# An attention and SwiGLU layer on one core: the paired P V of chunks 2 to 4 moved ahead by 10, 12 and 26 column blocks

## The chip, the cores and the metric

The kernel runs on one core of a Trainium2 chip. The metric is the device time of one execution in microseconds (us). The engines of the core are TensorE (PE in the profile, its weight loads PEld), VectorE (DVE), ScalarE (ACT), GpSimd (POOL) and SyncE (SP). Each works through its own list of instructions in order, and they wait for each other by semaphores. SP and ACT also issue DMA transfers, each through a queue of its own.

## The reference

The input x has 2048 rows of 576 values, in bf16. It is normalised once, and two branches read the result. The output is x plus both branches.

```python
xn = _layernorm(x)
# branch A: attention, H = 32 heads of Dh = 18, a window of W = 256 keys
qkv = (xn @ wqkv).reshape(B, S, 3, H, Dh)
scores = einsum("bhqd,bhkd->bhqk", q, k) * Dh ** -0.5
mask = (i - j >= 0) & (i - j < W)
A = einsum("bhqk,bhkd->bhqd", softmax(where(mask, scores, -1e9)), v) -> (B, S, D) @ wo
# branch B: gated MLP, F = 4608
h = silu(xn @ w1) * (xn @ w3)
B = h @ w2
return x + A + B
```

## The kernel before, in words

The 2048 rows are worked in four chunks of 512 (`CH`; the code counts them `c` = 0 to 3, the text 1 to 4). The 32 heads lie in eight groups of four (`G`). A chunk has these stages:

- **Units.** The loop `for u in range(NF)` (line 1391) makes 36 units of the gated MLP. A unit is 128 of the 4608 columns of gate and up. `unit_pairs` (line 851) issues it as nine **column blocks** (`for n in range(9)`, line 1399), each a pair of matmuls, one in each half of the array; one matmul reads `xnT`, or its copy with the halves swapped, `xnS`. Behind the nine blocks `unit_tanh` (ACT, line 869) and `unit_h` (two operations on DVE, lines 875 and 878) turn the two PSUM banks of the unit into a row block of `hT`. Three pairs of banks, handed out in turn by `job()`, serve the units.
- **Score steps among the units.** In chunks 2 to 4, attention groups 4 to 7 are worked here, five steps for a group, 20 in all. A step is `scores` (PE, line 682), `exps` (ACT, line 691) and `masks` (POOL, line 718). `spaced_step` (line 1367) sets them apart: a clock counts column blocks and steps, and the steps left share the blocks left up to `ALL_DONE[c]`, though never closer than 7.5. The exponentials lie in buffers: two slots of `stage`, the four buffers of W2 (`w2`), the slots `pt` and the buffers `od`.
- **The joint.** At block `n` of unit `u`, with `(u, n) = JOINTS[c]` (line 1401), both P V of the chunk are issued behind each other: `pv(c, 2, ...)` and `pv(c, 3, ...)` (line 739), 96 short matmuls each. They use the two pairs of banks that the current unit doesn't use. No score step falls in the eight blocks ahead (`calm`, line 1305), and all 20 steps must be done. The four transposes out of PSUM follow on DVE (`pv_out`, line 800), then the scaling on POOL (`o_scale`, line 806) and the transposes back (`o_turn`, line 813), dealt by `later` to the units `u` to `u + 5`. `o_pack` (line 817), four DMA issues on SP which wait for those transposes, moves the first pair into `oT` at `u + 3`; that of the second pair is put at `NF + 6` in chunks 2 and 3, and at `u + 6` in chunk 4.
- **W2's first pieces.** They go into the buffers `w2`, which hold exponentials until the first P V has read them. Line 1485 issues one in each of up to four units behind the joint, after that unit's last matmul:

```python
if joint[0] < u < joint[0] + 5:
    load_w2(c * 2 * NFC + 4, (op,))
```

- **Projections of the next chunk** (chunks 1 to 3, line 1504 on). `xn_swap` (line 460) copies `xnT` to `xnS` by two DMAs, once the last unit has read the old `xnS`; if fewer than four pieces of W2 have been issued, the rest is issued right behind it (line 1510). What `later` has dealt to units past the last comes out here, at item `m` for `u <= NF + m`. Then come the projections to queries, keys and values (`proj_part`, line 496), and the DMAs that deal them out: keys `new_k` on SP (line 638), queries `new_q` on ACT (four copies, line 625).
- **Lanes** (`w2_lanes`, chunks 1 to 3). The product with W2 runs in four row strips of the array at once (line 1036); among its rounds stand the score steps of the *next* chunk's groups 0 to 3 (line 756), which read `qv` and `kn`, and their P V (line 791). The first step is due 2.2 us into the stage (`W2_FIRST`). The last chunk has no next one and runs `p2_list` instead (line 932).

SP also loads the gate and up weights, a pair of parts at a time (`load_part`, line 343), by what the units owe: two parts behind every fourth unit, issued at blocks 3 and 8 of the unit that follows. In chunk 4 the last pair goes out in unit 24, and x of the chunk is loaded at unit 29 (`load_four`, line 315). The order of each engine's list is fixed when the program is written; nothing is chosen while it runs.

## Time and profile before

| | |
|---|---|
| median of three runs | 558.03 us (557.88 to 558.33) |
| the profiled execution's own time | 557.89 us |
| its span, from first to last instruction | 556.1 us |
| PE busy | 548.5 us (99%) |
| DVE, ACT, POOL busy | 364.5, 294.9, 120.4 us |
| time that PE's waits take by the list of waits | 1.8, 1.4, 1.2 and 0.6 us |
| start of the projections behind chunks 2 and 3 | 237.92 and 376.47 us |

A row of a timeline or of the chain gives the start in us from the start of the span, the length, the engine, the line of the kernel, the operation with `out<-in`, and how many were merged; in brackets stands the idle time just before it and what ended it. "issue" means that the engine waited for nothing that the profile shows. A row of a DMA view with 40 digits gives the busy share of the DMA engines in 40 equal slices of the stretch, in tenths. Queue q8 carries PE's instructions. A busy PE is a modelled figure, since matmuls overlap: the step from one row's start to the next is the better measure of pace.

### The profile page before, as it was taken

The numbers are of one execution on the slowest core, as the hardware profiler recorded it, in microseconds if no ns is written. First come the engines' busy times: TensorE is split into PE (matmuls) and PEld (weight loads), VectorE is DVE, ScalarE is ACT, GpSimd is POOL, SyncE is SP. The second block draws the span as 40 slices with busy tenths as digits, with TensorE's granted clock in tenths as the row PEclk, the third lists the DMA queues.
The fourth block names the chain that finished last, engine by engine and source line by source line (L and its number), as shares of the span: only waits on it lengthen the run. The fifth ranks groups of instructions, "written<-read, shape, count | busy, mean of one in ns | idle before, by whom it ended". The sixth has DMA issues, their size and how long they took to land.

```text
span 556.1 us, 17660 instructions
## 1 busy us (share of the span) xinstructions
PE 548.5 (99%) x7690; PEld 314.0 (56%) x7690; DVE 364.5 (66%) x745; ACT 294.9 (53%) x481; POOL 120.4 (22%) x281
## 2 busy tenths in 40 slices
PE   8999999999999999998999999999999999999998
PEld 4786554565564444565656444456555544444776
DVE  7566988746648787763665888676466676669011
ACT  6457766368826555246873565533786466533000
POOL 5524545100013422110001243202000232211000
PEclk9999999999999999999999999999999999999999
DMA  9997999559699999465979999937697989844552
GB/s 246 201 201 145 207 188 193 117 115 158 137 187 200 192 188 156 94 145 114 150 142 193 194 198 179 168 61 171 118 171 130 190 179 172 158 88 142 136 150 64
DMA packets 166070, 88.12 MB, mean 158 GB/s; under 512 B 101546, under 2 KB 163754, under 8 KB 165994
## 3 DMA queue, kind: packets, MB, share of 16 engines
q1 hardware_dynamic: 164622, 85.42, 81.2%
q10 hardware_dynamic: 1372, 1.59, 1.2%
q8 instruction: 60, 0.98, 0.8%
q14 instruction: 16, 0.13, 0.1%
HBM read 71.30 MB, written 2.36 MB: 132 GB/s over the span
## 4 chain that ended last, share of the span: by engine, by line
PE 98%; DMA 1%; issue 0%; ACT 0%; DVE 0%
PE ps L860 51%; PE ps L1036 16%; PE ps L496 9%; PE ps L932 6%; PE ps L682 4%; PE ps L1086 2%; PE ps L739 2%; PE ps L1045 2%; PE ps L756 2%; PE ps L791 2%; DMA qv<-stage 1%; PE ps L1160 1%; PE ps L939 1%; PE ps L1096 0%; PE ps L440 0%
## 5 line engine op out<-in xcount | busy, mean ns | idle before, releaser
L860 PE MATMUL ps<-xnT,w 64*128 64x512 bf16 x1400 | 179.3, 376 | 0.0
L860 PE MATMUL ps<-xnS,w 64*128 64x512 bf16 x1120 | 149.1, 376 | 0.6 <-issue 0.6
L875 DVE SCALAR_TENSOR_TENSOR gs<-thb,ps 128x512 bf16<-128x512 bf16 x144 | 97.8, 679 | 62.6 <-ACT thb L869 62.0
L869 ACT ACTIVATE thb<-ps 128x512 bf16<-128x512 f32 x144 | 85.7, 595 | 74.5 <-PE ps L860 72.9
L860 PEld LDWEIGHTS ps<-xnT,w 64*128 64x128 bf16 x1400 | 71.6, 94 | 67.4 <-DVE ofin L800 0.2
L1036 PE MATMUL ps<-hT,w 32*128 32x512 bf16 x1728 | 107.3, 374 | 0.0
L878 DVE SCALAR_TENSOR_TENSOR hT<-gs,ps 128x512 bf16<-128x512 bf16 x144 | 98.9, 687 | 5.0
L860 PEld LDWEIGHTS ps<-xnS,w 64*128 64x128 bf16 x1120 | 57.2, 94 | 55.7 <-issue 1.5
L1036 PEld LDWEIGHTS ps<-hT,w 32*128 32x128 bf16 x1728 | 59.3, 92 | 27.2 <-issue 1.4
L763 ACT ACTIVATE pt<-ps 128x512 bf16<-128x512 f32 x120 | 65.0, 595 | 9.8 <-PE ps L756 9.6
L691 ACT ACTIVATE pt<-ps 128x1024 bf16<-128x1024 f32 (+1 forms) x46 | 46.2, 1004 | 34.9 <-PE ps L682 34.8
L756 PE MATMUL ps<-qv,kn 18*128 18x384 bf16 (+2 forms) x288 | 54.6, 267 | 1.8 <-DMA qv<-stage 1.8
L806 POOL TENSOR_TENSOR oq<-uq,rden 128x288 bf16<-128x288 f32 x12 | 8.1, 672 | 189.4 <-DVE rden L805 189.4
L771 DVE TENSOR_TENSOR pt<-pt,kv 128x256 int32<-128x256 int32 x96 | 31.3, 371 | 26.6 <-ACT pt L763 26.1
L718 POOL TENSOR_TENSOR pt<-pt,mk 128x128 int32<-128x128 int32 (+1 forms) x82 | 33.1, 424 | 53.7 <-ACT pt L691 53.6
L496 PE MATMUL ps<-xnT,wp 64*128 64x512 bf16 (+1 forms) x360 | 38.5, 355 | 0.0
L932 PE MATMUL ps<-w,hT 128*128 128x288 bf16 (+1 forms) x292 | 36.9, 284 | 0.0
L756 PEld LDWEIGHTS ps<-qv,kn 18*128 18x128 bf16 x288 | 26.5, 93 | 16.7 <-issue 2.3
L932 PEld LDWEIGHTS ps<-w,hT 128*128 128x128 bf16 x292 | 28.2, 98 | 7.4 <-issue 0.5
L682 PE MATMUL ps<-qv,kv 64*128 64x320 bf16 (+4 forms) x336 | 32.1, 258 | 0.0
L813 DVE STREAM_TRANSPOSE od<-oq 128x256 bf16<-128x256 bf16 x64 | 25.5, 425 | 6.5 <-POOL oq L806 6.5
L990 DVE TENSOR_TENSOR thb<-ps,thb 128x512 f32<-128x512 f32 x24 | 16.6, 692 | 18.5 <-ACT thb L987 17.9
(132 smaller groups left out, 534.0 us busy)
## 6 DMA issues: line engine op xcount, KB each, us to landing
w<-in_B_w_dram SPq DMA_DIRECT2D x60, 576.0 KB, 7.5
w<-in_B_w_dram SPq DMA_DIRECT2D x72, 288.0 KB, 4.1
w<-in_B_w_dram SPq DMA_DIRECT2D x12, 192.0 KB, 6.8
xp<-in_A_x_dram SPq DMA_DIRECT2D x4, 576.0 KB, 5.0
xnS<-xnT SPq DMA_DIRECT2D x8, 256.0 KB, 4.8
xp<-in_A_x_dram SPq DMA_DIRECT2D x14, 144.0 KB, 4.4
oT<-od SPq DMA_DIRECT2D x56, 36.0 KB
w<-in_B_w_dram SPq DMA_DIRECT2D x6, 320.0 KB, 5.1
```

What stands on the lines that cost most here:

```text
L496: op = add("pe", lambda e, out_=out_, st=st, mv=mv, n=n, r0=r0, first=first: e.matmul(out_, st, mv, start=first, stop=(part == 1 and n == ...
L682: add("pe", lambda e, r0=r0, out_=out_, kb=kb, q0=q0, nb=nb: e.matmul(out_, kb4[r0:r0 + 64, g - GN, kb + NV - NB, :] if kb < 0 else kv[r0: ...
L691: add("act", lambda e: e.activation(pt_slot(sl)[:, 0:w, :], PS[:, SC[0]:SC[1] + 1, 0:w].rearrange("p r q -> p q r"), ACT.Exp, scale=scale) ...
L718: add("pool", lambda e, vb=vb, mm=mm: e.tensor_tensor(vb, vb, mm, ALU.mult), r=(key if n == 0 else []) + ["mk"], **{"w" if n == 0 else "j" ...
L756: add("pe", lambda e: e.matmul(PS[:, b, c0:c0 + nb * 128], kn[32 * a:32 * a + Dh, g, W + 128 * jb:W + 128 * jb + 128], qv[32 * a:32 * a + ...
L763: add("act", lambda e: e.activation(head_of(sl, p), PS[:, b, :], ACT.Exp, scale=scale), r=[("ps", b)], **{"j" if p else "w": pt_keys(sl)})
L860: op = add("pe", lambda e, n=n, r0=r0, r=r, k=k, src=src: e.matmul(PS[:, b0 + r, :], wt[r0:r0 + 64, k, fl * 128:(fl + 1) * 128], src, star ...
L869: add("act", lambda e: e.activation(th[i][:], PS[:, bg, :], ACT.Tanh, scale=0.5), r=[("ps", bg)], w=[("th", i)])
L875: add("dve", lambda e: e.scalar_tensor_tensor(out=gs[i][:], in0=th[i][:], scalar=1.0, in1=PS[:, bg, :], op0=ALU.add, op1=ALU.mult), r=[("t ...
L878: add("dve", lambda e: e.scalar_tensor_tensor(out=hT[:, u, :], in0=gs[i][:], scalar=0.5, in1=PS[:, bu, :], op0=ALU.mult, op1=ALU.mult), r= ...
L932: add("pe", lambda e: e.matmul(bank, hT[:, f, tt * 128:(tt + 1) * 128], w2[sl][:, k, n0:n1], start=first, stop=(c + 1 == NC and half == 1 ...
L1036: add("pe", lambda e, b=b, rows=rows, wt=wt, fl=fl, k=k, a=a, first=first: e.matmul(PS[:, b, :], wt[rows, fl, :], hT[rows, k, :], start=fi ...
```

## The change

The joints of chunks 2, 3 and 4 stand at other places, and the blocks by which the score steps are to be done with them. Chunk 1 is as before.

```diff
-        JOINTS = [(27, 6), (32, 7), (33, 8), (28, 6)]
-        AHEAD, ALL_DONE = 40, [0, 290, 298, 250]
+        JOINTS = [(27, 6), (31, 6), (32, 5), (25, 7)]
+        AHEAD, ALL_DONE = 40, [0, 276, 284, 215]
```

A unit has nine blocks, so (32, 7) to (31, 6) is 10 blocks, (33, 8) to (32, 5) is 12, and (28, 6) to (25, 7) is 26. Everything that is placed by the joint goes along: the P V pair, its transposes, scaling and `o_pack`, and W2's first pieces (units 32 to 35 in chunk 2, where it was 33 to 35; 33 to 35 in chunk 3, where it was 34 and 35; 26 to 29 in chunk 4, where it was 29 to 32). Pieces that the units leave out still follow the swap. The score steps stand closer: 20 steps in 276, 284 and 215 blocks.

## The prediction

> **What bounds the kernel now.** I read the page first, then TensorE's waits, then the stretches around the moved work.

> ```profile
> PE 548.5 (99%) x7690; PEld 314.0 (56%) x7690; DVE 364.5 (66%) x745; ACT 294.9 (53%) x481; POOL 120.4 (22%) x281
> q8 instruction: 60, 0.98, 0.8%
> ...
> L869 ACT ACTIVATE thb<-ps 128x512 bf16<-128x512 f32 x144 | 85.7, 595 | 74.5 <-PE ps L860 72.9
> ...
> L691 ACT ACTIVATE pt<-ps 128x1024 bf16<-128x1024 f32 (+1 forms) x46 | 46.2, 1004 | 34.9 <-PE ps L682 34.8
> ...
> PE ps L756 <- DMA qv<-stage: 1.8, 1, 1.8
> PE ps L739 <- issue: 1.4, 1, 1.4
> ...
> PE ps L860 <- issue: 0.6, 1, 0.6
> ```

> TensorE (PE) sets the time: busy 99%, and the change keeps every matmul. Only its gaps can move, and three touch this change: a wait for the query copies (L756), and two gaps in which PE waited for nothing that the profile shows: one inside P V (L739), one right behind it.

> The timelines of PE and its weight loads around the three joints (P V pairs) of chunks 2, 3 and 4:

> ```profile
> 228.97 0.32 PE L739 MATMUL ps<-stage,va 64*20 64x320 bf16 x4
> ...
> 231.43 0.39 PE L860 MATMUL ps<-xnS,w 64*128 64x512 bf16 x2
> 231.66 1.24 PE L860 MATMUL ps<-xnT,w 64*128 64x512 bf16 x10
> 232.74 1.45 PE L860 MATMUL ps<-xnS,w 64*128 64x512 bf16 x8
> 233.82 0.38 PE L860 MATMUL ps<-xnT,w 64*128 64x512 bf16 x1
> ...
> 371.51 1.35 PE L860 MATMUL ps<-xnT,w 64*128 64x512 bf16 x10
> 373.45 1.04 PE L860 MATMUL ps<-xnS,w 64*128 64x512 bf16 x8 [0.60 <-issue]
> ...
> 499.06 0.09 PEld L739 LDWEIGHTS ps<-pt,va 64*20 64x20 bf16 x4 [1.55 <-issue]
> ```

> Ten block matmuls normally step 1.08 us (231.66 to 232.74), so eight should step 0.86. In chunk 2 eight took 1.08: **0.22 lost**. In chunk 3 ten took 1.94: **0.86 lost**. In chunk 4 the idle is **1.55**. Sum 2.63 us.

> What stops PE there? Queue q8 brought 60 blocks of 16 KB; the page counts 7690 matmuls and 7690 weight loads, so a block is about 256 PE instructions. Counts of instructions from each P V's start to its stop, and between two stops (columns: window, its length, then busy time and count of PE, of PEld, of the others):

> ```profile
> 372.80:497.90 125.10, 124.31 (x1909) 67.64 (x1907) 81.62 (x166) 72.94 (x122) 21.80 (x51) 1.00 0.82 153
> 228.97:232.96 3.99, 3.99 (x209) 3.00 (x207) 3.22 (x7) 0.60 (x1) 0.67 (x1) 1.00 0.02 4
> 369.04:372.50 3.46, 3.46 (x204) 2.93 (x203) 2.48 (x6) 0.56 (x1) 0.53 (x1) 1.00 0.02 5
> 495.28:497.50 2.22, 2.22 (x186) 2.11 (x184) 1.64 (x4) 0.00 (x0) 0.00 (x0) 1.00 0.03 7
> ```

> Between the two stops lie 3816 instructions, 14.9 blocks; with the two dozen separate waits among them that is 15. So PE stops at a block's edge, out of instructions. Counting off the one or two still running at a window's start, the edge stands 414, 405 and 369 instructions behind the P V's start in chunks 2, 3, 4. And in the stretch 496.7 to 499.0 the DMA view has a single packet, of q8, in the second of 40 slices:

> ```profile
> DMA  0900000000000000000000000000000000000000
> ```

> It starts at 496.8; PE resumes at 499.06, 2.3 us later.

> **The change part by part.** *The P V pair.* Two P V are 384 instructions (192 matmuls and their loads) in 2.46 us (228.97 to 231.43): 6.4 ns each. The column blocks take 1.08/20 = 54 ns per instruction, a unit of 36 1.94 us. PE asks for a block at about the time when it enters the one before. Chunk 2 ran its block in 226x6.4 ns + 30x54 ns = 3.07 us and lost 0.22; chunk 3 in 235 and 21: 2.64, lost 0.86; chunk 4 wholly inside P V: 1.64, lost 1.55. So a fetch needs 3.2 to 3.5 us: three places, one number. All score steps still stand ahead of the P V, so its start moves by its column blocks alone, four instructions each: 40, 48, 104 sooner. The edges then lie at:
> - chunk 2: 58 ahead, 198 and 454 behind the start: blocks of 4.40 and 4.97 us;
> - chunk 3: 59, 197, 453: 4.45 and 4.92 us;
> - chunk 4: 39, 217, 473: 3.50 and 5.88 us.

> All exceed or reach 3.5, where an idle DMA serves the fetch. The gain is between 0 and 2.63. What can hold a fetch up is the gate/up weights' traffic. DMA views of 365.5 to 367.0, of 486.5 to 487.7 (its only packet) and of 486 to 496, and the pieces issued then:

> ```profile
> DMA  3691321010101000000000000000000000000000
> ...
> 486.97 1.68 SPq L343 DMA_DIRECT2D w<-in_B_w_dram  x2
> ...
> q8 instruction: 1, 0.02, 4.8%
> ...
> DMA  1020000005596699999999999999999985000000
> ```

> Chunk 3's first edge stands now 107 instructions (5.8 us) ahead of the P V, at 363; its packet started at 365.6 (third slice), when that traffic ended. The new P V starts 12 blocks (2.6 us) sooner, at 366.4, and needs this block 59 instructions behind the same edge and 1.27 us into the P V, at 367.7; the packet is usable 2.3 us behind its start, 367.9, and the traffic may be a score step (0.4) later: 0 to 1.1 lost, taken as 0.4. In chunk 4 a fetch starts at 486.6 (third slice), ahead of the weights' burst of 488.3 to 494.5, which ends 6 us behind its second issue (1.68 us for both). The pieces will go out some 2.4 and 1.2 us ahead of the P V; a fetch for the second edge, held to the burst's end (5 us into the P V), is usable at 7.3, needed at 1.39 + 5.88 = 7.3: 0 to 0.8 with the same step's lateness, taken as 0.3. Of the 2.63 I leave 0.7 lost.

> [...]

> *Banks.* P V's second half takes the banks of the unit ahead. VectorE's last read of them in chunk 3 ends 0.43 us into the P V, which stands behind eight blocks of its unit:

> ```profile
> 368.78 0.69 DVE L878 SCALAR_TENSOR_TENSOR hT<-gs,ps 128x512 bf16<-128x512 bf16 x1
> ```

> Behind five (joint 32,5) it ends 3x0.216 = 0.65 later, at 1.08, against 192x6.4 ns = 1.23: free by 0.15, or 0.1 lost to the semaphore. The unit behind the P V waits less for its banks with more blocks between. I put 0.05.

> *Score steps.* Their PE work only changes place. The tightest spacing is chunk 4's, (215-8)/20 = 10.35 blocks = 2.2 us instead of 12.1; ACT needs 1.00 for the exponentials and 0.60x2.2/1.94 for the tanh: 1.7. Covered; without that cover up to 0.5 per step. VectorE and POOL do as much per unit as before.

> *W2's pieces, and the query copies behind them.* SP's queue is in order. Per chunk it issues W2 pieces in the units behind the joint, the pack of oT three units behind it (waits for VectorE), the swap of xnS at the start T of the projections, and the key copies; ACT issues the query copies. Chunk 2 first (PE, ACT, DVE and SP rows, and the chain's), then chunk 3:

> ```profile
> 237.92 5.34 PE L496 MATMUL ps<-xnT,wp 64*128 64x512 bf16 x46
> 238.34 0.44 DVE L813 STREAM_TRANSPOSE od<-oq 128x256 bf16<-128x256 bf16 x1
> 234.44 2.32 SPq L379 DMA_DIRECT2D w<-in_B_w_dram  x2
> 238.81 3.09 SPq L817 DMA_DIRECT2D oT<-od  x4
> 241.94 0.47 SPq L379 DMA_DIRECT2D w<-in_B_w_dram  x1
> 242.52 1.19 SPq L460 DMA_DIRECT2D xnS<-xnT  x2
> 243.76 0.75 SPq L379 DMA_DIRECT2D w<-in_B_w_dram  x1
> 248.88 6.63 DMA qv<-stage
> 255.76 0.21 PE L756 MATMUL ps<-qv,kn 18*128 18x128 bf16 x1 [1.82 <-DMA qv<-stage]
> ...
> 376.47 5.14 PE L496 MATMUL ps<-xnT,wp 64*128 64x512 bf16 x46
> 374.74 2.33 SPq L379 DMA_DIRECT2D w<-in_B_w_dram  x2
> 377.18 1.41 SPq L460 DMA_DIRECT2D xnS<-xnT  x2
> 378.62 2.20 SPq L379 DMA_DIRECT2D w<-in_B_w_dram  x2
> 387.35 0.73 ACTq L625 DMA_DIRECT2D qv<-stage  x1
> 392.21 0.22 PE L756 MATMUL ps<-qv,kn 18*128 18x128 bf16 x1
> ```

> From T, chunk 2 issues the pack at 0.9 to 4.0 (right behind the transpose that follows unit 34), so the third piece, the swap and the fourth piece come late, the last at 6.6 (T is 237.92). Then the fourth query copy takes 6.63 us and PE waits 1.82. Chunk 3, its pack due at u = 36 and hence behind the swap, has its bulk out by 4.35 (T is 376.47): the copy lands within 392.21-387.35 = 4.86 us, no wait.

> With joint 31 chunk 2 issues two pieces in units 32 and 33, the pack a unit sooner (-1.05 to 2.05), pieces three and four, and the swap from 3.2 to 4.4. On a line between (4.35, no wait) and (6.6, 1.82) its wait is 0.04; bounds 0 and 1.82. I take 0. With joint 32 chunk 3 gets word for word the order that chunk 2 has now: pieces in 33 and 34, pack in 35 held by the transpose behind unit 34, swap, fourth piece at 6.6. I take chunk 2's 1.82; bounds 0 and 1.82. **The wait moves from chunk 2 to chunk 3: net 0.** Chunk 4's pieces and the load of x behind its first ones are ten units ahead of their use (19 us).

> *Sum.* 557.89 (the profiled execution: span 556.1 and 1.8 around it) - 2.63 + 0.7 + 0.05 - 1.82 + 1.82 = 556.0; the median is 0.14 above the profiled run: **556.1**.

> **The rivals.**
> 1. *The query wait goes from both chunks*: chunk 2's as above, and chunk 3's copies land in time because their packets fall otherwise on the DMA engines. For it: chunk 3 now has 4.86 us without a wait. Against: its order becomes that of the waiting chunk. 556.1-1.8 = 554.3.
> 2. *Chunk 2 keeps its wait*, chunk 3 gains one: the pack still stands ahead of the swap. 556.1+1.8 = 557.9.
> 3. *The gaps move with the P V*: they are not fetches at the edges, or the fetches are held as long behind the gate/up weights, of which chunk 3's packet is an instance. 557.89 with nothing of the 2.63 gained, the query wait changing place: 558.0. Against: three places give one fetch time.
> 4. *Slower: chunk 4's fetch behind the last gate/up pieces.* The block needed 1.39 us into the P V is asked for about 2 us ahead of it; if its packet starts behind the burst's first packets (about 1 us ahead of the P V), it waits to 5 and is usable at 7.3: 5.9 lost, where I have none. 556.1+5.9 = 562.0. The point is whether the request beats the burst. For it: chunk 3's packet did wait for such a burst. Against: the fetch that now serves this very block starts at 486.6, 1.7 us ahead of the burst.

> **How the numbers follow.** Forecast 0.52, rival 1 0.17, rival 2 0.10, rival 3 0.11, rival 4 0.10. Faster or slower begins at 0.2% (1.1 us), what a measurement can tell here. Faster: rival 1 and most of the forecast (its fetches at their worst, 1.9 lost, give 557.3), 0.63; same: rivals 2, 3 and that rest, 0.26; slower 0.11. The range 554.0 to 558.2 holds the forecast and rivals 1 to 3 and leaves rival 4 out; the forecast's own is 555.4 to 557.3.

> **What would show it.** Right: no issue gap of over 0.8 us at L739 or behind it in the three joints; the L756 wait at about 392 minus some 4 us and none near 254; chunk 3's pack ahead of its swap on SP. Wrong: an issue gap of several us inside chunk 4's P V with its q8 packet at the end of the weights' burst (rival 4); two L756 waits (2) or none (1); gaps of the old size at new places (3).

## The result and the profile after

The changed kernel takes 556.0 us in the median of 12 executions (553.53 to 556.66), the kernel before 557.92 us (12, 557.2 to 560.8). The ratio is 0.995, with a 95% interval of 0.9932 to 0.9968: 1.8 to 3.8 us faster. The forecast was 556.1. The two profiled executions took 557.89 and 555.12 us. Two single executions far off all others (985 us at a clock of 0.61, and 3296 us) are left out of the ratios of the experiments.

The page and the list of TensorE's waits of the changed kernel:

```profile
PE 547.7 (99%) x7690; PEld 305.0 (55%) x7690; DVE 365.2 (66%) x745; ACT 294.2 (53%) x481; POOL 120.0 (22%) x281
...
PE ps L1160 <- DVE oq L1154: 1.2, 1, 1.2
PE ps L739 <- issue: 1.1, 2, 0.6
PE ps L756 <- DMA qv<-stage: 0.5, 1, 0.5
PE ps L496 <- ACT xnT L447: 0.5, 1, 0.5
```

The query wait is down from 1.8 to 0.5 us, and the largest issue gap from 1.4 to 0.6. Where that happened is seen when the span is cut at the first matmul of each stage. First the kernel before, then the changed one. The columns are the stretch, its length, then busy time and count of PE, PEld, DVE, ACT, POOL, PE's granted clock (1.00 is full), the DMA share and GB/s. The stretches are chunk 1's units, the projections and lanes behind them, the same for chunks 2 and 3, and chunk 4 to the last matmul.

```profile
21.12:102.08 80.96, 80.96 (x1085) 49.35 (x1079) 63.48 (x118) 52.27 (x71) 31.10 (x74) 1.00 1.03 185
102.08:160.81 58.73, 58.73 (x1095) 35.48 (x1085) 34.21 (x84) 36.20 (x72) 4.05 (x8) 1.00 0.74 136
160.81:237.92 77.11, 77.07 (x945) 37.38 (x939) 60.84 (x115) 39.95 (x55) 21.43 (x52) 1.00 0.93 166
237.92:298.72 60.80, 58.98 (x1087) 39.22 (x1084) 33.94 (x84) 36.77 (x73) 4.05 (x8) 1.00 0.79 144
298.72:376.47 77.75, 77.15 (x944) 37.80 (x938) 60.87 (x114) 39.95 (x55) 21.70 (x52) 1.00 0.87 162
376.47:435.11 58.64, 58.64 (x1086) 35.23 (x1084) 34.19 (x85) 36.79 (x73) 4.05 (x8) 1.00 0.80 152
435.11:553.52 118.41, 117.06 (x1280) 68.98 (x1272) 63.40 (x113) 40.33 (x56) 19.76 (x46) 1.00 0.67 142
```

```profile
21.03:102.60 81.57, 81.00 (x1084) 42.28 (x1080) 63.40 (x118) 52.27 (x71) 30.16 (x74) 1.00 1.03 182
102.60:161.32 58.72, 58.72 (x1095) 35.19 (x1085) 34.20 (x84) 36.20 (x72) 4.06 (x8) 1.00 0.73 138
161.32:238.25 76.93, 76.93 (x945) 37.40 (x938) 61.76 (x117) 39.73 (x55) 22.12 (x53) 1.00 0.94 170
238.25:296.81 58.56, 58.56 (x1087) 35.18 (x1084) 33.17 (x82) 36.79 (x73) 3.38 (x7) 1.00 0.74 144
296.81:374.56 77.75, 77.18 (x944) 37.36 (x938) 61.79 (x115) 39.84 (x55) 21.62 (x52) 1.00 0.92 167
374.56:433.86 59.30, 58.78 (x1088) 37.94 (x1084) 33.86 (x84) 36.77 (x73) 4.05 (x8) 1.00 0.77 147
433.86:550.82 116.96, 116.96 (x1278) 68.95 (x1272) 63.15 (x113) 40.01 (x56) 19.56 (x46) 1.00 0.67 143
```

| stage | before | after | difference | what it is |
|---|---|---|---|---|
| chunk 1's units | 80.96 | 81.57 | +0.61 | the same program; a gap that comes and goes (below) |
| chunk 2's units | 77.11 | 76.93 | -0.18 | the gap behind its P V pair |
| projections and lanes behind chunk 2 | 60.80 | 58.56 | -2.24 | its query wait (2.06 in the lanes), and 0.18 in the projections |
| chunk 3's units | 77.75 | 77.75 | 0.00 | one gap for another |
| projections and lanes behind chunk 3 | 58.64 | 59.30 | +0.66 | a new query wait |
| chunk 4 | 118.41 | 116.96 | -1.45 | the gap inside its P V pair |

The stages that the change touches gain 3.2 us. Chunk 1's units have the same instructions in every version without added ones, and their profiles take from 80.7 to 83.2 us. Part of that is of the kind studied here: the list above has two issue gaps at L739, and one of them, 0.57 us at 54.15, stands inside a P V of chunk 1. The two longest (83.0 and 83.2 us) have besides waits of 1.2 and 1.8 us for the DMA `kv<-stage`. None of it comes from the change, so the small parts below are read from stages, not from whole times.

In chunk 2 SP's queue and PE's first score step of the changed kernel are these (the projections start at 238.25):

```profile
236.99 3.08 SPq L817 DMA_DIRECT2D oT<-od  x4
240.12 1.11 SPq L379 DMA_DIRECT2D w<-in_B_w_dram  x2
241.33 1.73 SPq L460 DMA_DIRECT2D xnS<-xnT  x2
...
249.04 0.73 ACTq L625 DMA_DIRECT2D qv<-stage  x1
253.91 0.22 PE L756 MATMUL ps<-qv,kn 18*128 18x128 bf16 x1
```

The pack starts ahead of the projections, the swap is out 4.8 us behind their start, and the first score step runs without a wait.

In chunk 3 the P V pair starts at 364.5. The changed kernel's PE timeline there, and SP's queue, the chain and PE at the projections and the lanes behind it:

```profile
366.57 0.64 PE L739 MATMUL ps<-pt,va 64*20 64x320 bf16 x32 [0.57 <-issue]
...
374.56 5.13 PE L496 MATMUL ps<-xnT,wp 64*128 64x512 bf16 x46
370.87 2.32 SPq L379 DMA_DIRECT2D w<-in_B_w_dram  x2
375.25 3.08 SPq L817 DMA_DIRECT2D oT<-od  x4
378.37 0.47 SPq L379 DMA_DIRECT2D w<-in_B_w_dram  x1
378.95 1.19 SPq L460 DMA_DIRECT2D xnS<-xnT  x2
380.19 0.72 SPq L379 DMA_DIRECT2D w<-in_B_w_dram  x1
385.35 5.30 DMA qv<-stage
390.89 0.21 PE L756 MATMUL ps<-qv,kn 18*128 18x128 bf16 x1 [0.52 <-DMA qv<-stage]
```

SP's order is the forecast one: pack, third piece, swap, fourth piece, the last out 6.35 us behind the start of the projections (374.56). The fourth query copy took 5.30 us, where chunk 2's had taken 6.63 under the same order, so PE waited 0.52 instead of 1.82.

### The profile page after: what moved, and what is told of

Same layout as the page of the kernel before. It is cut to its first block, busy times and chain, and to the rows that moved or that the text cites. A ratio compares the mean times of both kernels' runs of the same rounds, so it can differ in the third digit from the quotient of the medians.

```text
span 553.4 us, 17660 instructions
## 1 busy us (share of the span) xinstructions
PE 547.7 (99%) x7690; PEld 305.0 (55%) x7690; DVE 365.2 (66%) x745; ACT 294.2 (53%) x481; POOL 120.0 (22%) x281
## 4 chain that ended last, share of the span: by engine, by line
PE 98%; DMA 1%; issue 0%; ACT 0%; DVE 0%
PE ps L860 51%; PE ps L1036 16%; PE ps L496 9%; PE ps L932 6%; PE ps L682 4%; PE ps L1086 2%; PE ps L739 2%; PE ps L1045 2%; PE ps L791 2%; PE ps L756 2%; DMA qv<-stage 1%; PE ps L1160 1%; PE ps L939 1%; PE ps L1096 0%; PE ps L440 0%
## 5 line engine op out<-in xcount | busy, mean ns | idle before, releaser
L860 PE MATMUL ps<-xnT,w 64*128 64x512 bf16 x1400 | 177.3, 376 | 0.0
L860 PE MATMUL ps<-xnS,w 64*128 64x512 bf16 x1120 | 147.5, 376 | 0.0
L869 ACT ACTIVATE thb<-ps 128x512 bf16<-128x512 f32 x144 | 85.7, 595 | 78.3 <-PE ps L860 76.8
L860 PEld LDWEIGHTS ps<-xnT,w 64*128 64x128 bf16 x1400 | 67.1, 94 | 70.3 <-issue 0.4
L878 DVE SCALAR_TENSOR_TENSOR hT<-gs,ps 128x512 bf16<-128x512 bf16 x144 | 98.9, 687 | 5.0
L860 PEld LDWEIGHTS ps<-xnS,w 64*128 64x128 bf16 x1120 | 54.0, 94 | 58.1 <-issue 0.2
L691 ACT ACTIVATE pt<-ps 128x1024 bf16<-128x1024 f32 (+1 forms) x46 | 46.2, 1004 | 33.9 <-PE ps L682 33.9
L756 PE MATMUL ps<-qv,kn 18*128 18x384 bf16 (+2 forms) x288 | 54.6, 267 | 0.5 <-DMA qv<-stage 0.5
L496 PE MATMUL ps<-xnT,wp 64*128 64x512 bf16 (+1 forms) x360 | 38.1, 355 | 0.0
L756 PEld LDWEIGHTS ps<-qv,kn 18*128 18x128 bf16 x288 | 26.6, 93 | 14.7 <-issue 1.0
L682 PE MATMUL ps<-qv,kv 64*128 64x320 bf16 (+4 forms) x336 | 31.7, 258 | 0.0
L813 DVE STREAM_TRANSPOSE od<-oq 128x256 bf16<-128x256 bf16 x64 | 25.4, 425 | 5.5 <-POOL oq L806 5.5
```

What stands on the lines that cost most here:

```text
L496: op = add("pe", lambda e, out_=out_, st=st, mv=mv, n=n, r0=r0, first=first: e.matmul(out_, st, mv, start=first, stop=(part == 1 and n == ...
L682: add("pe", lambda e, r0=r0, out_=out_, kb=kb, q0=q0, nb=nb: e.matmul(out_, kb4[r0:r0 + 64, g - GN, kb + NV - NB, :] if kb < 0 else kv[r0: ...
L691: add("act", lambda e: e.activation(pt_slot(sl)[:, 0:w, :], PS[:, SC[0]:SC[1] + 1, 0:w].rearrange("p r q -> p q r"), ACT.Exp, scale=scale) ...
L756: add("pe", lambda e: e.matmul(PS[:, b, c0:c0 + nb * 128], kn[32 * a:32 * a + Dh, g, W + 128 * jb:W + 128 * jb + 128], qv[32 * a:32 * a + ...
L860: op = add("pe", lambda e, n=n, r0=r0, r=r, k=k, src=src: e.matmul(PS[:, b0 + r, :], wt[r0:r0 + 64, k, fl * 128:(fl + 1) * 128], src, star ...
L869: add("act", lambda e: e.activation(th[i][:], PS[:, bg, :], ACT.Tanh, scale=0.5), r=[("ps", bg)], w=[("th", i)])
```

## The experiments

### The edges moved, the joints left in place

Three edits at the start of the program put short warming matmuls in place of ten long ones. Each is two PE instructions, a weight load and a matmul (with 84 for ten the page counts 7764 of each, 7690 before), so every block edge moves against the P V's. Queue q8 brought 60 packets of 16 KB for 15380 such instructions, and 61 both with 128 and with 148 more.

```diff
 # the kernel before, 148 more
-        warm(4, *[CH] * 10)
+        warm(4, *[128] * 84)
 # the changed kernel, 128 more; a third one has 89 here, 158 more
-        warm(4, *[CH] * 10)
+        warm(4, *[128] * 74)
```

> The changed kernel with 128 more PE instructions at the start (74 warming matmuls of 128 columns for ten of 512); the joints stay at their new places. Theory of the edges: they move from 198, 197 and 217 behind the P V's start to 70 and 326, 69 and 325, 89 and 345, a whole block inside each P V. Lost 1.6 us or more in each of chunks 2, 3 and 4, more where the gate/up weights' traffic still holds the fetch (chunk 4 up to 5, since its burst lasts until some 5 us into the P V). Total 3 to 8 us above the changed kernel, 559 to 564. Rival (the gaps were removed by the P V's new place): nothing new, 556 plus or minus 1.

It took 575.2 us (ratio to the kernel before 1.031, 95% interval 1.0286 to 1.0327; the intervals below are of the same kind). Counts from each P V's start to the stop in it, and PE's rows where it resumes:

```profile
237.44:239.60 2.16, 2.16 (x165) 1.95 (x164) 1.57 (x4) 0.00 (x0) 0.00 (x0) 1.00 0.55 89
376.54:378.70 2.16, 2.16 (x164) 1.96 (x163) 1.78 (x4) 0.00 (x0) 0.00 (x0) 1.00 0.04 9
500.96:503.10 2.14, 2.14 (x174) 2.04 (x173) 1.37 (x3) 0.00 (x0) 0.00 (x0) 1.00 1.14 241
...
241.39 0.22 PE L739 MATMUL ps<-pt,va 64*20 64x128 bf16 x1 [1.72 <-issue]
380.25 0.23 PE L739 MATMUL ps<-pt,va 64*20 64x128 bf16 x2 [1.49 <-issue]
508.69 0.23 PE L739 MATMUL ps<-od,va 64*20 64x64 bf16 x4 [5.47 <-issue]
```

Less the one or two that still run at a window's start, the stops stand 326, 324 and 345 instructions behind the start, where the theory had put the edges. In chunk 4 the P V starts while the weights' burst runs (DMA share 1.14 in the row): the packet of the fetch starts at 506.0, when that burst ends, and 5.5 us are lost where up to 5 was expected. The joints stand where the changed kernel has them: so the gaps go with the edges, and the rival falls. The total is beyond the 3 to 8 us expected, because a P V pair of chunk 1 was hit too (6.4 us in one gap), and because of the clock (last section).

> The kernel before with 148 more PE instructions at the very start (the ten warming matmuls of 512 columns become 84 of 128, about the same 4.5 us); no joint moves. Theory (PE runs out of instructions at the edges of blocks of 256 when a block is used up in less than some 3.4 us): all edges move 148 instructions nearer to the P V's start. Chunk 2 has them 10 and 266 behind it, chunk 3 1 and 257, so a whole block lies inside the P V: about 1.6 us lost in each, at the edge 266 and 257 behind the start (0.22 and 0.86 before). Chunk 4 has them at -35, 221 and 477: blocks of 3.3 and 6.1 us, so about nothing lost where 1.55 was. Sum 3.2 against 2.63: total time within 1 us of before, the start apart. Rival (the gaps belong to the P V's place among the other work): they stay at 0.22, 0.86 and 1.55. The query wait stays in chunk 2 alone, about 1.8 us, under both.

The stops in chunks 2 and 3 did not appear: both pairs ran through in 2.46 us though each holds a whole block. Chunk 4's gap of 1.55 us was gone as expected, all but one step of 0.32 us at the edge 221 behind the start.

```profile
239.32:241.78 2.46, 2.46 (x194) 2.24 (x193) 1.69 (x3) 0.00 (x0) 0.00 (x0) 1.00 0.00 0
378.29:380.75 2.46, 2.46 (x195) 2.24 (x194) 1.48 (x3) 0.00 (x0) 0.00 (x0) 1.00 0.03 7
```

The total (ratio 1.012, 1.0098 to 1.014), expected within 1 us of before, rose by chunk 1, where a 6.4 us gap opened and the units took 89.8 us. The miss in chunks 2 and 3 fits a request for the next block that goes out before execution enters the one ahead of it: there the q8 packet starts 0.9 and 1.5 us ahead of the edge. With the edge 9 or 0 instructions into the P V such a request falls into the slow stretch ahead of it, at 54 ns an instruction, and gains 2 us, an estimate for some 40 instructions. The third edit places the edge in between:

> The changed kernel with 158 more PE instructions at the start (89 warming matmuls of 128 columns for ten of 512), which puts edges 40 and 296 behind the P V's start in chunk 2 and 39 and 295 in chunk 3. What it tells: how far ahead of the running instruction the next block is asked for. With 148 more on the kernel before (edges 9 and 265) nothing was lost, with 128 more on the changed one (70 and 326) 1.9 and 1.7. If the block is asked for when execution enters the block ahead, 1.6 to 2.0 lost at 296 and 295. If it is asked for some 50 instructions ahead, the request falls before the P V, in the slow stretch: 1.0 to 1.4 lost; some 64 ahead: 0.4 to 0.8. In chunk 4 (59 and 315) 1.5 to 5 under all, by the weights' burst.

```profile
239.35 0.33 PE L739 MATMUL ps<-pt,va 64*20 64x64 bf16 x8 [1.48 <-issue]
377.53 0.34 PE L739 MATMUL ps<-pt,va 64*20 64x64 bf16 x9 [0.80 <-issue]
505.31 0.44 PE L739 MATMUL ps<-od,va 64*20 64x320 bf16 x3 [5.14 <-issue]
```

From matmul to matmul that is 1.67 us lost in chunk 2 and 1.00 in chunk 3, against 1.94 and 1.70 with the edge at 70 and nothing at 9 and 0. Taken alone the two disagree: 1.67 lies in the range of a request at the moment of entry, 1.00 in that of one 50 instructions ahead. With the run above, where nothing was lost, they fit a request some 45 to 55 instructions ahead and a fetch time that varies by some tenths, both estimates from these losses.

The packets of the fetches show it without a fetch time. Compare the start of the q8 packet with the start of the matmul where the count puts the edge. In the kernel before, the packet starts 0.8 to 0.9 us behind the edges 113, 149 and 158. In the three runs of this section it starts 0.5 us behind the edges 70 and 69, 0.4 and 0.2 behind 40 and 39, but 0.9 and 1.5 us ahead of 9 and 0 (chunks 2 and 3). A request 48 instructions ahead of the edge and 1.1 us from there to the packet give 0.8 behind, 0.8, 0.4, then 1.1 and 1.5 ahead. Both figures are estimates, fitted to these packets, with 54 ns for an instruction ahead of the P V and 6.4 inside it.

The total is 571.3 us (one execution), with 5.1 us lost in chunk 4 by the burst.

### What holds the fetch in chunk 3

> The changed kernel, but in chunk 3 the last pair of gate/up weight parts (for the next chunk) is issued in unit 33, behind the joint, instead of unit 28. Theory (that burst holds the fetch for the edge 197 instructions into chunk 3's P V): with DMA idle there, the packet starts no more than 1 us behind the edge ahead of the P V and the gap inside the P V (0.87 us at the 98th matmul) is gone. In exchange the pair falls together with W2's pieces and the swap, and PE's wait for the query copies in chunk 3 grows beyond the 0.5 of the changed kernel, to 2 us or more. Rival (the fetch is slow by itself): packet still 2 to 3 us behind the edge, gap as before.

```diff
-                if u == 27 and c + 1 < NC:
+                if u == (32 if c == 2 else 27) and c + 1 < NC:
```

The only packet between 358 and 366 is the fetch (DMA view, 40 slices), at 358.8; in the changed kernel's trace it starts at 363.9:

```profile
DMA  0000200000000000000000000000000000000000
...
q8 instruction: 1, 0.02, 0.7%
```

It starts 1.85 us ahead of the edge instead of 2.6 behind it, the gap is gone, and chunk 3's units take 76.90 us instead of 77.75. The query and key copies then kept PE 0.5 and 0.7 us in the list of waits, and the lanes took 1.7 us more than where nothing waits (46.96 against 45.28 us), a little under the 2 expected: what the gap gave was lost again. The total is 554.9 us (one execution).

The weights' burst does hold the fetch, though not in every execution. In the ten other profiles without added instructions, where the burst stands in its place, the packet for the first edge ahead of chunk 3's P V starts 0.1 to 2.8 us behind that edge, in seven of them over 2. The second profile of the changed kernel, below, is one of the other three: there the packet starts in the middle of the burst, 0.9 us behind the edge, and no gap follows.

### The order on SP

The pack of the first pair goes behind the swap and the pieces, in the changed kernel and in the kernel before:

```diff
-  later(u + 3, lambda ...: (o_pack(ja, "sp"), o_turn(g + 2, 0), o_turn(g + 2, 1), o_scale(3)))
+  later(NF if 0 < c < NC - 1 else u + 3, lambda ja=ja: o_pack(ja, "sp"))
+  later(u + 3, lambda ...: (o_turn(g + 2, 0), o_turn(g + 2, 1), o_scale(3)))
```

> The kernel before with the pack of chunks 2 and 3 behind swap and pieces, the joints at their old places. Theory (SP's order makes the query wait): PE's wait for the query copies in chunk 2 (0.9 to 2.0 us in the four profiles that have the old joint) is gone though the joint has not moved; the issue gaps of 0.2, 0.9 and 1.6 us stay. 1 to 2 us faster than before. Rival (moving the joint itself removed the wait, by the PE and DVE work that it moves): the wait stays.

```profile
240.19 1.19 SPq L460 DMA_DIRECT2D xnS<-xnT  x2
241.41 0.85 SPq L379 DMA_DIRECT2D w<-in_B_w_dram  x1
242.31 3.56 SPq L817 DMA_DIRECT2D oT<-od  x4
...
252.77 2.55 PE L1036 MATMUL ps<-hT,w 32*128 32x512 bf16 x44
255.16 0.22 PE L756 MATMUL ps<-qv,kn 18*128 18x128 bf16 x1
```

The pack now follows swap and piece, the first score step runs 2.4 us into the lanes without a wait, and the joint hasn't moved. The gaps in chunks 3 and 4 stayed (0.4 and 1.3 us in PE's list); chunk 2's, of 0.2 us before, is not in this profile (with the joint at its old place its length varies, from 0 to 0.3 us in four profiles). The ratio is 0.9969 (0.9956 to 0.9982), 1.0 to 2.5 us faster: as expected, and the rival falls.

> The changed kernel, but in chunks 2 and 3 the first pair's pack of oT is issued on SP behind the swap of xnS and W2's pieces instead of three units behind the joint. Theory (the query copies are late because the pack, which waits for VectorE, holds back swap and pieces on SP): chunk 3's bulk is out by about 2 us behind the start of the projections instead of 6.4, the wait of PE for the query copies in chunk 3 (0.5 us in the changed kernel's profile) is gone, chunk 2 stays without. 555.0 to 555.5 median and a narrower spread, if the spread of the changed kernel (553.5 to 556.7) comes from this wait. Rival (the copies' time is set by their own packets and the key copies beside them): the wait stays, no difference in time.

Its profile has no query wait in either chunk. The time is 555.4 us, ratio 0.9945 (0.9924 to 0.9966), which can't be told from the changed kernel's. The spread (552.7 to 555.9) is no narrower; the profiled execution, the longest of the six, has 83.2 us in chunk 1's units, as said above.

### The parts alone

Each has one chunk's joint and `ALL_DONE` of the change, the rest as before.

> Of the change only chunk 2's part: joint (31, 6), steps done by 276. Theory: pack, W2's pieces and swap are all out by some 4.7 us behind the start of the projections, PE's wait for the query copies in chunk 2 (1.8 us before) is gone, and with it the 0.2 us gap behind the P V. Chunks 3 and 4 as before, with their issue gaps of 0.9 and 1.6 us. About 2 us faster than before, 555.4 to 556.2, less what chunk 1 varies by (0 to 2 us between executions in the profiles so far). Rival (the copies are late whatever stands ahead of them): wait stays over 1 us, no change in time.

The ratio is 0.9985 (0.9963 to 1.0007). The profile has neither the wait nor the gap in chunk 2: its units take 76.91 us, and the lanes behind it 45.28, the same as behind the others. Issue gaps of 1.4 (L739) and 0.7 us (L860) stayed in chunks 4 and 3. By stages 2.4 us were gained; whole times show 0.8, with an interval that reaches from -0.4 to 2.1, so the 2 us expected stand at its edge.

> Of the change only chunk 3's part: joint (32, 5) and steps done by 284, chunks 2 and 4 as before. Theory: chunk 3's order on SP becomes that of chunk 2, so a second wait for query copies of 0.5 to 1.8 us appears in chunk 3, beside chunk 2's 1.8. The issue gap of 0.86 behind the P V is gone, but one of about 0.86 stands inside it at the edge 197 behind its start, since the fetch waits for the gate/up weights' traffic. Slower than before by 0.5 to 1.8 us: 558.4 to 559.8. Rival (chunk 3's part is a gain by itself): 0.8 us faster.

The ratio is 1.0008 (0.9986 to 1.003): no difference, where 0.5 to 1.8 us slower was expected. Its profile has the gap at the 98th matmul (0.86 us between two matmuls), but a query wait behind chunk 3 of 0.1 us only.

> Of the change only chunk 4's part: joint (25, 7), steps done by 215. Theory: the edges stand 217 and 473 behind the P V's start instead of 113 and 369; the gap inside the P V (1.6 us) is gone; at 473, 44 matmuls behind the P V, 0 to 0.8 us is lost, since the weights' burst holds that fetch. The stage from chunk 4's first unit to the end takes 117.0 to 117.6 us instead of 118.4. Total 1 to 1.5 us faster than before. Rival (the first edge's fetch falls behind the burst): a gap of several us inside the P V, slower than before.

The ratio is 0.9981 (0.9965 to 0.9997), 0.2 to 2.0 us faster. Chunk 4 took 117.33 us. 44 matmuls behind the P V stands one step of 0.47 us where 0.21 is normal: 0.26 lost. All of this is as expected.

### A version with both ideas, and the changed kernel again

```diff
-        JOINTS = [(27, 6), (31, 6), (32, 5), (25, 7)]   # and 284
+        JOINTS = [(27, 6), (31, 6), (32, 8), (25, 7)]   # and 287, the pack behind
```

> The changed kernel with the pack behind swap and pieces in chunks 2 and 3, and chunk 3's joint three blocks later, (32, 8), steps done by 287. The edges stand 71 ahead, 185 and 441 behind the P V's start; the block up to the first takes 5.0 us, 0.5 more than at (32, 5). Theory (the fetch for it starts 2.2 to 3.1 us behind the edge, held by the gate/up weights, and is usable 2.6 later): the gap inside chunk 3's P V (0 to 0.9 us) shrinks to 0 to 0.7, and no query wait in chunks 2 and 3. 554.8 to 555.8. Rival (the gap has nothing to do with where the edge stands): 0.9 us at the same 98th matmul.

> Pack behind swap and pieces in chunks 2 and 3, chunk 3's joint at (32, 8). Theory: no query wait, no gap inside chunk 3's P V, so 0.5 to 1.5 us faster than the changed kernel on the same chip, all of it in the stages from chunk 3's units to the lanes behind them.

> The changed kernel unchanged, beside the next two for a comparison on one chip and as a second profile of it. Theory: in chunk 3 a query wait of 0.1 to 0.7 us and a gap of 0 to 0.9 us inside the P V, at the 98th matmul if there is one; none of either in chunk 2; at most 0.6 us 44 matmuls behind chunk 4's P V. Ratio to the kernel before 0.994 to 0.997.

The version took 554.6 and 554.8 us (0.9948, 0.9932 to 0.9965; 0.9947, 0.9932 to 0.9962); the changed kernel, measured together with the second, 554.7 (0.9954, 0.9936 to 0.9972). Neither profile of the version has a query wait or a gap in PE's list inside chunk 3's P V. What is left of the gap is one step, of 0.16 us in the first and 0.17 in the second, 92 matmuls into the P V. The count puts the edge there (185 instructions), and at joint (32, 5) it stood at the 98th: the gap moves with the edge, and this rival falls too. But the changed kernel's second profile has no wait and no gap either: its units of chunk 3 take 76.90 us and the lanes behind them 45.29, as when nothing waits. Both losses in chunk 3 are there in some executions and not in others, and the version gains nothing that these runs can tell, where 0.5 to 1.5 us was expected.

## Why the prediction was right, and where it was not

**What bounds.** Right: PE's matmuls take the same time in the stages that wait for nothing (58.56 to 58.73 us in the four stretches of projections and lanes without a wait, two in each list above), and all of the difference is gaps.

**The edges.** Right in place: with 128 instructions added PE stops where the count puts the edges, and with the joint at its new place and no added instruction the gaps of chunks 2 and 4 are gone (0.22 and 1.55 us forecast, 0.18 and 1.45 found). The step "PE asks for a block at about the time when it enters the one before" failed: by the estimates above the request goes out some 45 to 55 instructions sooner (about 48 by the packets). For edges well inside the P V the fetch time read from the three old gaps hides that, since 50 instructions of P V are 0.3 us; for an edge at its start it is worth 2 us, as the run with 148 more showed. The new joints' first edges stand ahead of the P V, so there the failed step could only make the forecast too careful.

**What still holds a fetch.** The sum left 0.4 us for chunk 3 and 0.3 for chunk 4. Chunk 3 lost 0.85 (77.75 against 76.90) in the profile beside the forecast, inside the 0 to 1.1 given, and nothing in the second profile. Chunk 4 lost 0.1 to 0.6 in the seven profiles with its new joint and no added instructions (one step of 0.30 to 0.83 us where 0.21 is normal). The reason given, the weights' burst, was shown in chunk 3 by moving it; in chunk 4 the packet starts 3.1 to 3.7 us behind the edge 217 instructions into the P V in all seven, with the burst running up to it, but no run moved the burst there.

**Banks and score steps.** Right: no wait for either appears in PE's list. VectorE's last read of the banks in chunk 3 ends 1.07 us into the P V, where 1.08 was worked out.

**The query wait.** Right for chunk 2: nothing waits there in any profile with joint (31, 6), and the pack's place on SP is the cause, shown on the kernel before by moving the pack alone. Wrong for chunk 3: "I take chunk 2's 1.82". PE's list shows 0.5, 0.2 and nothing in the profiles of that order, where chunk 2 had 1.8, 1.1, 0.7 and 1.5 under the same order. The order came out as said; its price did not carry over. Why chunk 2 pays more for it than chunk 3 stays open; both vary between executions, and no run here told the two chunks apart.

**The sum.** The forecast has 0 net for the query wait and 1.9 us for the gaps. The profiles give 1.6 for the wait with the projections ahead of it (-2.24 and +0.66) and 1.6 for the gaps (0.18, 0.00, 1.45), 3.2 together. So the wait's term was too small by 1.6 us and the gaps' too large by 0.3; in the two profiled executions chunk 1's 0.6 went the other way. That the median still came within 0.1 us of the forecast is luck: the medians contain all of these parts, and they vary by more than that from one execution to the next.

**Rivals.** Of the first, the query wait gone from both chunks, the second profile is an instance. The second, chunk 2 keeps its wait, is in none of the nine profiles with joint (31, 6). Of the third, chunk 3 in the first profile is an instance in its second form: the gap goes along with the P V (0.86 us before, 0.85 after), now because the weights' burst holds the fetch. The slower one did not occur in the changed kernel, but its mechanism and price did when the edge was moved into the burst: 5.5 us against the 5.9 worked out.

## What to carry to other kernels

Where a run of short matmuls is longer than a block of instructions (384 against about 256 here), count in which block it starts: an edge a little ahead of it and one in its middle (58 ahead, 198 behind the start) cost nothing here while no other traffic held the fetch, and up to 0.9 us where a burst did. Two edges inside it cost 1 to 2 us, and 4 to 6 beside a burst; only with the first one 0 or 9 instructions into it, and no burst, did they cost nothing. Instructions added ahead move all of them: 128 at the start of the program put stops 326, 324 and 345 instructions behind the three starts. On an in-order queue that issues DMAs, an issue that waits for another engine belongs behind those that are ready and that somebody needs soon; on SP in the kernel before that was worth 1.0 to 2.5 us.

## What the runs showed of the hardware that was not expected

Long gaps inside a P V cost more than their length. The three kernels with added instructions have five of them: 6.4 and 5.5 us with 128 more, 6.4 with 148, 3.7 and 5.1 with 158. The rows are of the changed kernel with 128 more instructions, chunk 4: the gap, the time behind it, and what follows (the column behind the five engines is PE's granted clock).

```profile
503.20:508.60 5.40, 0.02 (x6) 0.00 (x0) 0.62 (x2) 0.00 (x0) 0.67 (x1) 0.84 0.56 97
508.90:514.50 5.60, 5.60 (x49) 2.02 (x32) 3.51 (x7) 1.09 (x2) 0.67 (x1) 0.58 0.02 3
515.00:520.00 5.00, 5.00 (x50) 2.24 (x46) 4.68 (x10) 1.36 (x3) 0.67 (x1) 1.00 0.48 125
```
